# A prologue reordered in a Nyström attention and two-layer feed-forward kernel: query scores first, one weight quarter in two halves, one subtraction on another engine

## The chip, the cores and the metric

The kernel runs on one core of one Trainium2 chip. The metric is the time on the device in microseconds, and of several runs the median counts. The core has five engines that matter here: TensorE (PE in the profile, PEld for its weight loads), VectorE (DVE), ScalarE (ACT), GpSimd (POOL) and SyncE (SP), which issues the DMAs.

## What is computed

Three stages follow each other: Nyström attention over 4 batches of 8 heads (576 tokens of 64 values each), a SiLU layer with 2048 inner values, and a gated layer with RMS norm and 1536 inner values. The weights come as float64 and are turned into float32 on the chip.

```python
def _attn_ref(q, k, v):                      # m = 32 landmarks
    q_lm = q.reshape(B, H, m, S // m, D).mean(axis=3)
    k_lm = k.reshape(B, H, m, S // m, D).mean(axis=3)
    A = sm(q, k_lm)
    Bm = sm(q_lm, k_lm)
    C = sm(q_lm, k)
    Z = Bm.transpose(0, 1, 3, 2) / (norms of Bm + 1e-06)
    for _ in range(6):
        Z = 2 * Z - Z @ Bm @ Z
    return (A @ Z @ C @ v).astype(np.float32)

h = x @ w_in;  x = (h * sigmoid(h)) @ w_out
xn = x / rms * rms_g
out = (silu(xn @ w_gate) * (xn @ w_val)) @ w_out2
```

`sm` is a softmax of 0.125 times the product of its arguments, each row less its maximum.

## The kernel before, in words

**What is multiplied.** For each batch and each group `g` of four heads the attention makes two things: `at`, which is A (split into a rounded high part and a low part), and `lt`, a small 64 x 128 block that is Z, C and v multiplied out. The function `wprime(b, n)` multiplies `lt` into quarter `n` of w_in (512 columns), which gives the quarter `n` of the weights "wp" of that batch; the products `h` (L641) take `wp` and `at`. So nothing of the large products can start before `lt` of both groups of batch 0 is there, the first quarter of w_in is in float32, and `wprime(0, 0)` has run. That stretch of some 39 us is the prologue. After it PE runs the products `h` and `a` of the first layer, then the second layer.

**The prologue's attention.** `attention(ap, b, g, first)` is a generator; each `yield` ends a step. The two generators a0 and a1 (the two groups of batch 0, `first` true) are advanced in turn by the loop at the end of the function, a1 two steps behind a0. A step is: load q and k; load v; POOL sums the landmarks of q (L275 to L279); DVE sums those of k (`landmarks`, two TENSOR_REDUCE of kT, one for each half i); the key scores `pq` (L301, with k's landmarks as weights, needing all of q) and their transposes on DVE into `sa`; the query scores `c2` and then `c1` (L301, with q's landmarks as weights, needing all of k and its landmarks), six filler matmuls behind them for a1 (`idle`, L240), then the key maximum `ms` on DVE and the subtraction on POOL (L352); the query maximum on DVE (`mx`, then `nb`); the exponentials `bb` and `ec` on ACT; sums and reciprocals; `p1`, the norm and the first `rt`, and the transposes `ct` of `ec` (L408); copies of `ct`, the exponential of `sa`, and its sums; `pu` (L425), the rest of `rt`, and `sa` scaled on POOL (L429); six iterations `pe` (L308), each with a copy back (by DVE for a0, by ACT for a1) and a filler; at last `pl` and `lt` (DVE). In iteration 1 DVE transposes `sa` into `sb`, in iteration 2 ACT rounds it into the high part of `at`, in iteration 3 POOL subtracts that for the low part (L458).

**The conversion of w_in.** `load_win(n, g)` loads one quarter of one group (1 MB of float64) and `to_f32` converts it in blocks of 512 values: two ACT instructions (L163, L164) and two DVE instructions (L168, L170) a block, so eight and eight for the first quarter. Of L168 and L170 both inputs lie in SBUF, as both inputs of L458, L429 and L352 do. `load_wout(f)` does the same for a row block of w_out.

**What sets the order.** The framework puts each engine's instructions in one order at compile time, by program order shifted by `high_priority(offset)`, by a model of when each can run, and by `issue_after`, which keeps an instruction behind another on its engine. Each engine then runs its list in order. The dictionary `CONV` says behind which step t of the prologue's loop a conversion goes on (before: steps 11 to 20; entry 0 and 1 are the two groups' w_in, 2 is the first block of w_out). DMAs go to SP's queue in program order: q and k of both groups, w_in of group 0, v of both groups, w_in of group 1, four blocks of w_out, the second quarter of w_in.

**After the attention.** `wprime(0, 0)` issues its 16 matmuls (L478, two passes of 8, 512 columns), six fillers, and then in cuts of 256 columns ACT rounds `wp` (L486) and DVE subtracts (L487). Behind its last subtraction come the rest of the conversions of w_out's first four blocks, then w_in's second quarter, which `wprime(0, 1)` needs after the fifth step of the first layer.

Of the kernel before, what the change touches and what calls it, by code (L numbers as in the profile page):

```python
# [45 lines left out]
CONV = {11: (0,), 13: (0, 1), 14: (0,), 15: (0,), 16: (0, 2), 17: (1,), 18: (1,), 19: (1,), 20: (1,)}  # L46
# [20 lines left out]
def nystrom_moe_kernel(ctx: ExitStack, tc: tile.TileContext, q, k, v, w_in, w_out, w_gate, w_val, w_out2, rms_g, out):  # L67
# [130 lines left out]
    def load_win(n, g):  # L198
        raw = wslot(f"winr_{g}_{n}", [P, 2, 1024], I32)
        SP.dma_start(out=raw, in_=win_v[g, n].rearrange("c p f -> p c f"))  # L200
        yield
        t = nslot(2 * n + g, f"win_{g}_{n}", [P, 2, 512])
        size = (512, 512) if n < 2 else (1024, 1024)
        yield from to_f32(t.rearrange("p c f -> p (c f)"), raw.rearrange("p c f -> p (c f)"), *size)
        win_t[g, n] = t

# [35 lines left out]
    def attention(ap, b, g, first):  # L242
# [92 lines left out]
        sa = ht("sa", [P, R, M])  # L335
        for hf in range(2):
            pq = pa.tile([P, HB], F32, tag="a", name=f"pq_{n}_{hf}") if first else ps(f"pq_{n}_{hf}", [P, HB])
            scores(pq, kT, qT, 9 * hf, 9 * hf + 9)
            VE.transpose(sa[:, 9 * hf:9 * hf + 9].rearrange("p r j -> p (r j)"), pq)
        yield  # L340

        r1 = 10
        c1 = ps(f"c1_{n}", [P, r1 * M])
        c2 = ps(f"c2_{n}", [P, (R + 1 - r1) * M])
        for ci, (lo, hi) in ((c2, (r1, R + 1)), (c1, (0, r1))):
            x = scores(ci, qT, kT, lo, hi)
        if first and g:
            idle(x, 6)
        ms = sm("ms", [P, R])
        msb = ms.unsqueeze(2).to_broadcast([P, R, M])  # L350
        VE.tensor_reduce(ms, sa, axis=AX.X, op=ALU.max)
        (POOL if b <= POOL_B else VE).tensor_tensor(sa, sa, msb, op=ALU.subtract)  # L352
        yield
        nc2 = (R - r1) * M
        mx = sm("mx", [P, 4])
        nb = sm("nb", [P, 2])
        VE.tensor_reduce(mx[:, 2:3], c2[:, nc2:], axis=AX.X, op=ALU.max)
        VE.tensor_scalar(nb[:, 1:2], mx[:, 2:3], -0.125 / R ** 2, None, op0=ALU.mult)
        VE.tensor_reduce(mx[:, 1:2], c2[:, :nc2], axis=AX.X, op=ALU.max)
        VE.tensor_reduce(mx[:, 0:1], c1, axis=AX.X, op=ALU.max)  # L360
        VE.tensor_scalar(nb[:, 0:1], mx[:, 0:1], mx[:, 1:2], -0.125 / R, op0=ALU.max, op1=ALU.mult)
        yield
        ec = ht("ec", [P, M, R])
        ecv = ec.rearrange("p l r -> p r l")
        bb = sm("bb", [P, 2, M])
        su = sm("su", [P, 3])
        with ExitStack() as es:
            if first:
                es.enter_context(tc.high_priority(offset=EXP_PRIO))
                AE.activation(bb[:, 0], c2[:, nc2:], AF.Exp, bias=nb[:, 1:2], scale=0.125 / R ** 2, accum_out=su[:, 2:3])  # L370
                AE.activation(ecv[:, r1:], c2[:, :nc2].rearrange("p (r l) -> p r l", l=M), AF.Exp, bias=nb[:, 0:1], scale=0.125 / R, accum_out=su[:, 1:2])
                AE.activation(ecv[:, :r1], c1.rearrange("p (r l) -> p r l", l=M), AF.Exp, bias=nb[:, 0:1], scale=0.125 / R, accum_out=su[:, 0:1])
            else:
                es.enter_context(tc.issue_after(now[-1][0].ins))
                x = AE.activation(ecv[:, r1:], c2[:, :nc2].rearrange("p (r l) -> p r l", l=M), AF.Exp, bias=nb[:, 0:1], scale=0.125 / R, accum_out=su[:, 1:2])
                with tc.issue_after(x.ins):
                    AE.activation(bb[:, 0], c2[:, nc2:], AF.Exp, bias=nb[:, 1:2], scale=0.125 / R ** 2, accum_out=su[:, 2:3])
                    AE.activation(ecv[:, :r1], c1.rearrange("p (r l) -> p r l", l=M), AF.Exp, bias=nb[:, 0:1], scale=0.125 / R, accum_out=su[:, 0:1])
                    AE.activation(sa, sa, AF.Exp, scale=0.125 / R)
        yield  # L380
# [50 lines left out]
        for it in range(6):  # L431
# [38 lines left out]
    def wprime(b, nb_, prio=0):  # L470
# [4 lines left out]
        for i in range(4):  # L475
            for g in range(NG):
                hr = slice(64 * g, 64 * g + 64)
                x = PE.matmul(pw[g][32 * i:32 * i + 32], lts[b][hr, i], win_t[i // 2, nb_][hr, i % 2], start=True, stop=True)  # L478
        if (b, nb_) == (0, 0):
            idle(x, 6)  # L480
# [426 lines left out]
    early = [load_win(0, g) for g in range(NG)] + [load_wout(f) for f in range(EARLY)] + [load_win(1, g) for g in range(NG)]  # L907
    for gn in (a0, a1, early[0], a0, a1, *early[1:]):
        next(gn)
    t = 0  # L910
    live = [a0]
    while live:
# [4 lines left out]
        for n in CONV.get(t, ()):  # L917
            with tc.issue_after(VE.last.ins), tc.issue_after(AE.last.ins):
                next(early[n], None)
    with tc.issue_after(VE.last.ins):  # L920
        for gn in early[:NG]:
# [9 lines left out]
    with tc.issue_after(AE.last.ins):  # L931
        next(early[NG])
        for gn in early[NG + 1:NG + EARLY]:
            next(gn)
    z = wprime(*todo.pop(0), WP_PRIO)
    with tc.issue_after(z.ins):
        for gn in early[NG:NG + EARLY]:
            finish(gn)
    jobs = {f"n1{g}": gn for g, gn in enumerate(early[NG + EARLY:])}
# [196 lines left out]
```

## Time and profile before

| what | us |
|---|---|
| median of 3 runs (lowest, highest) | 881.53 (880.26, 884.51) |
| the profiled execution | 879.2 |
| its span in the profile | 877.4 |
| PE busy | 843.8 (96%) |
| DVE busy | 510.0 (58%) |
| ACT busy | 440.6 (50%) |
| POOL busy | 147.6 (17%) |

Busy shares are averages over stages with different limits. PE is near its limit over the whole span, and less so in the first 39 us, where it does small matmuls and fillers. A line of the timeline reads: start, duration, engine, line of the kernel, operation, output and inputs by the program's names, shape, how many instructions are merged, and in brackets how long the engine sat idle before it and what ended that.

### The profile page before, as it was taken

What the parts mean: (1) busy time and instruction counts of PE and PEld (TensorE: products, weight loads), DVE (VectorE), ACT (ScalarE), POOL (GpSimd) and SP (SyncE); (2) the same over time, 40 slices, a digit from 0 to 9 for tenths busy, and PEclk for the clock granted to TensorE, in tenths of its full rate; (3) what the DMA queues carried; (4) which work ended last, traced back from release to release, by engine and by line L of the source; (5) the groups of instructions that cost most, each with busy time, mean ns of one, the idle gap of its engine ahead of it and who ended that gap; (6) DMA issues with size and microseconds to landing.
All of it is one profiled execution on the core that took longest, in us unless ns stands there. A gap on an engine that the chain in (4) does not pass through costs nothing.

```text
span 877.4 us, 15413 instructions
## 1 busy us (share of the span) xinstructions
PE 843.8 (96%) x5896; PEld 735.9 (84%) x5896; DVE 510.0 (58%) x1038; ACT 440.6 (50%) x906; POOL 147.6 (17%) x171
## 2 busy tenths in 40 slices
PE   6899999999988999899989999999999999999996
PEld 3667766988876889889979888999989999999995
DVE  6878736786557647649853569733458434333332
ACT  3796523776556757656653346633445323232222
POOL 5200210223231222163740003300000000000000
PEclk9999999999998999999999999999999999999999
DMA  9788647128886569986895456758645557655543
GB/s 317 278 302 306 236 163 218 57 85 270 289 268 197 150 207 349 329 311 242 307 398 201 183 200 208 273 219 305 228 174 213 216 216 256 235 198 190 194 186 72
DMA packets 72586, 202.85 MB, mean 231 GB/s; under 512 B 6593, under 2 KB 34241, under 8 KB 68545
## 3 DMA queue, kind: packets, MB, share of 16 engines
q1 hardware_dynamic: 72512, 201.88, 65.4%
q8 instruction: 46, 0.75, 0.3%
q14 instruction: 28, 0.22, 0.1%
HBM read 149.29 MB, written 52.56 MB: 230 GB/s over the span
## 4 chain that ended last, share of the span: by engine, by line
PE 79%; DMA 6%; DVE 6%; ACT 5%; issue 2%; POOL 1%; SPq 0%; ACTq 0%; DVEq 0%; POOLq 0%
PE ga L815 17%; PE o L889 17%; PE a L661 11%; PE h L641 10%; PE gc L815 8%; PE a L658 7%; PE gb L815 4%; PE pw L478 2%; DMA w7d<-w7p 2%; PE pe L308 1%; DMA r_o<-in_moe_w_out_dram 1%; DMA r_v<-in_moe_w_val_dram 1%; DMA w<-w7d 1%; PE pq L301 1%; DVE lms L179 1%
## 5 line engine op out<-in xcount | busy, mean ns | idle before, releaser
L889 PE MATMUL o<-oc,u 128*128 128x512 f32 x648 | 178.9, 394 | 0.0
L661 PE MATMUL a<-hl,wo 128*128 128x288 f32 x1152 | 171.7, 298 | 2.5 <-DVE e L689 1.9
L815 PE MATMUL ga<-x,w 128*128 128x384 f32 x840 | 171.2, 338 | 2.3 <-DMA w<-w7d 1.2
L815 PEld LDWEIGHTS ga<-x,w 128*128 128x128 f32 x840 | 150.8, 188 | 16.6 <-ACT a L179 2.0
L661 PEld LDWEIGHTS a<-hl,wo 128*128 128x128 f32 x1152 | 159.8, 190 | 4.4 <-ACT hl L145 2.1
L641 PE MATMUL h<-at,wp 128*128 128x288 f32 x768 | 134.3, 310 | 3.3 <-ACT s L648 2.4
L641 PEld LDWEIGHTS h<-at,wp 128*128 128x128 f32 x768 | 110.1, 190 | 27.4 <-issue 7.8
L889 PEld LDWEIGHTS o<-oc,u 128*128 128x128 f32 x648 | 118.9, 188 | 13.0 <-DVE u L146 0.3
L179 DVE TENSOR_TENSOR v<-u,gc 128x384 f32<-128x384 f32 x72 | 39.6, 551 | 120.7 <-PE gc L815 120.5
L815 PE MATMUL gc<-x,w 128*128 128x384 f32 x420 | 84.8, 336 | 0.0
L815 PEld LDWEIGHTS gc<-x,w 128*128 128x128 f32 x420 | 74.8, 188 | 3.1
L146 POOL TENSOR_TENSOR hl<-s,hl 128x288 fp32r<-128x288 f32 x54 | 48.4, 898 | 146.6 <-ACT hl L145 120.6
L179 ACT COPY u<-ga 128x384 f32<-128x384 f32 x72 | 34.5, 479 | 71.4 <-PE ga L815 71.1
L179 DVE TENSOR_TENSOR u<-z,v 128x384 f32<-128x384 f32 x72 | 40.3, 560 | 50.9 <-ACT z L179 50.0
L658 PE MATMUL a<-s,wor 128*128 128x288 f32 x256 | 69.8, 409 | 0.0
L145 ACT CAST u<-u 128x384 fp32r<-128x384 f32 x72 | 36.9, 513 | 65.1 <-DVE u L179 65.1
L648 ACT ACTIVATE s<-h 128x288 f32<-128x288 f32 x96 | 38.9, 409 | 53.1 <-PE h L641 50.8
L146 DVE TENSOR_TENSOR u<-u,u 128x384 fp32r<-128x384 f32 x72 | 40.1, 557 | 29.6 <-ACT u L145 29.3
L658 PEld LDWEIGHTS a<-s,wor 128*128 128x128 f32 x256 | 45.8, 189 | 11.9 <-issue 1.7
L179 ACT ACTIVATE z<-ga 128x384 f32<-128x384 f32 x36 | 17.7, 492 | 73.9 <-PE ga L815 73.7
L551 POOL TENSOR_TENSOR t<-fw 128x256 f32<-128x256 f32 x24 | 22.7, 965 | 139.0 <-ACT x L779 81.4
L815 PE MATMUL gb<-x,w 128*128 128x384 f32 x210 | 42.3, 335 | 0.8 <-DVE v L179 0.8
(175 smaller groups left out, 1069.3 us busy)
## 6 DMA issues: line engine op xcount, KB each, us to landing
w<-w7d SPq DMA_DIRECT2D x31, 1792.0 KB, 7.3
oc<-wod SPq DMA_DIRECT2D x32, 512.0 KB, 7.9
win<-wind SPq DMA_DIRECT2D x20, 512.0 KB, 6.6
fw<-w2d SPq DMA_DIRECT2D x12, 768.0 KB, 6.8
winr<-in_moe_w_in_dram SPq DMA_DIRECT2D x8, 1024.0 KB, 7.0
wor<-in_moe_w_out_dram SPq DMA_DIRECT2D x16, 512.0 KB, 7.0
w7d<-w7p SPq DMA_DIRECT2D x16, 512.0 KB, 5.4
r_v<-in_moe_w_val_dram SPq DMA_DIRECT2D x12, 512.0 KB, 4.4
```

The lines of the kernel that those rows point to most:

```text
L145: x = ACT.copy(dst[:, 0], src) if hi is ACT else hi.tensor_copy(dst[:, 0], src)
L146: return x, lo.tensor_tensor(dst[:, 1], src, dst[:, 0].bitcast(F32), op=ALU.subtract)
L179: self.last = getattr(self.eng, name)(*args, **kw)
L301: x = PE.matmul(out[o], lm[y, i, R], t[y, i, lo:hi], start=True, stop=True)
L478: x = PE.matmul(pw[g][32 * i:32 * i + 32], lts[b][hr, i], win_t[i // 2, nb_][hr, i % 2], start=True, stop=True)
L551: POOL.tensor_tensor(t[:, to], x, y, op=ALU.subtract)
L641: PE.matmul(ph, w[:, x, fo:fo + P], a[:, y, tk], start=i == 0, stop=i == 5)
L648: ACT.activation(s, ph, AF.Silu)
L658: PE.matmul(acc[d], w[:, y], hl, start=start, stop=stop)
L661: PE.matmul(acc[d], w[:, x, y], hl[:, z], start=start and i == 0, stop=stop and i == 2)
L815: mm[0] = PE.matmul(acc, w7[:, x, o, kk], xs[:, y, kk], start=start and n == 0, stop=stop and n == 5, skip_group_check=True)
L889: PE.matmul(oacc[n], hls[j][:, x, t * P:(t + 1) * P], w[:, y], start=f == 0 and i == 0, stop=f == NF2 - 1 and i == 2)
```

## The change

In the attention of the first batch the query scores, their maximum (at high priority) and their exponentials come first, and the key scores, their transposes and their maximum behind them; a step less is needed. The subtraction for the low part of `at` (L458) goes from POOL to DVE for batch 0 (for batch 1 it stays on POOL, and later batches have it on DVE already). The first quarter of w_in is loaded in four DMAs of 256 of its 512 columns each, the first halves of both groups ahead of v and the second halves behind it, and it is converted in these halves, from step 8 to step 16 of a loop that is a step shorter; the ACT part of the first half stands ahead of the loop. `wprime(0, 0)` does the matmuls, the rounding and the subtraction for the first 256 columns and then for the others, with the six fillers between. The first DVE instruction on w_out's first block (L168) goes from ahead of `wprime(0, 0)` to behind it. Batches 1 to 3 keep the order of their scores.

```diff
-CONV = {11: (0,), 13: (0, 1), 14: (0,), 15: (0,), 16: (0, 2), 17: (1,), 18: (1,), 19: (1,), 20: (1,)}
+CONV = {8: ((1, 0),), 9: ((0, 0),), 10: ((0, 0),), 11: ((1, 0), (0, 1)), 12: ((1, 0), 0), 13: ((0, 1), (1, 1)), 14: ((0, 1),), 15: ((1, 1),), 16: ((1, 1),)}
...
+    def load_win0(x):
+        for g in range(NG):
+            if not x:
+                raw0.append(wslot(f"winr_{g}_0", [P, 2, 1024], I32))
+                win_t[g, 0] = nslot(g, f"win_{g}_0", [P, 2, 512])
+            y = slice(2 * x, 2 * x + 512)
+            SP.dma_start(out=raw0[g][:, :, y], in_=win_v[g, 0].rearrange("c p f -> p c f")[:, :, y])
+
+    def conv_win0(g, x):
+        raw, c = raw0[g][:, :, 2 * x:2 * x + 512], win_t[g, 0][:, :, x:x + 256]
...
+        ACT.activation(c, hi.bitcast(F32), AF.Abs, scale=2.0 ** -112)
+        ACT.activation(lo, raw.bitcast(U16).rearrange("p c (f t) -> p c f t", t=4)[:, :, :, 1], AF.Copy, scale=2.0 ** -13, bias=2.0 ** -14 - 0.5)
+        yield
+        DVE.scalar_tensor_tensor(out=lo, in0=hi, scalar=-0x80000000, in1=lo, op0=ALU.bitwise_and, op1=ALU.bitwise_or)
+        yield
+        DVE.scalar_tensor_tensor(out=c.bitcast(I32), in0=c.bitcast(I32), scalar=3, in1=lo, op0=ALU.logical_shift_left, op1=ALU.bitwise_or)
...
+        if first:
+            c1, c2, x = query_scores()
+            if g:
+                idle(x, 6)
+            with tc.high_priority(offset=EXP_PRIO):
+                query_max()
+            yield
+            with tc.high_priority(offset=EXP_PRIO):
+                ec, bb = exps()
+            key_scores()
+            yield
+            key_max()
+            yield
...
-                (POOL if b <= POOL_B else VE).tensor_tensor(at[:, 1], sb, at[:, 0].bitcast(F32), op=ALU.subtract)
+                (POOL if b == POOL_B else VE).tensor_tensor(at[:, 1], sb, at[:, 0].bitcast(F32), op=ALU.subtract)
...
         cut = W0 if (b, nb_) == (0, 0) else 512
-        with tc.high_priority(offset=prio):
-            for x in range(0, 512, cut):
-                y = slice(x, x + cut)
+        for x in range(0, 512, cut):
+            y = slice(x, x + cut)
+            for i in range(4):
+                for g in range(NG):
+                    hr = slice(64 * g, 64 * g + 64)
+                    z = PE.matmul(pw[g][32 * i:32 * i + 32, y], lts[b][hr, i], win_t[i // 2, nb_][hr, i % 2, y], start=True, stop=True)
+            if cut < 512 and not x:
+                idle(z, 6)
+            with tc.high_priority(offset=prio):
                 for g in range(NG):
                     ACT.copy(t[:, g, 0, y], pw[g][:, y])
                     z = DVE.tensor_tensor(t[:, g, 1, y], pw[g][:, y], t[:, g, 0, y].bitcast(F32), op=ALU.subtract)
...
-    for gn in (a0, a1, early[0], a0, a1, *early[1:]):
+    next(a0)
+    next(a1)
+    load_win0(0)
+    next(a0)
+    next(a1)
+    load_win0(256)
+    for gn in early:
         next(gn)
+    halves0 = {(g, x): conv_win0(g, 256 * x) for g in range(NG) for x in range(2)}
+    next(halves0[0, 0])
...
-        next(early[NG])
-        for gn in early[NG + 1:NG + EARLY]:
+        for gn in early[1:EARLY]:
             next(gn)
```

## Rows read from the trace of the kernel before

**Rows 1.** The page, busy time of each engine (share of the span) and instructions.
```profile
PE 843.8 (96%) x5896; PEld 735.9 (84%) x5896; DVE 510.0 (58%) x1038; ACT 440.6 (50%) x906; POOL 147.6 (17%) x171
```

**Rows 2.** The chain that ended last, first 70 us: start, us, what.
```profile
27.40 1.65 DVE winr L168
...
31.33 1.82 DVE wor L168
```

**Rows 3.** Timeline, 6 to 12 us: landmarks and the scores of a0.
```profile
6.56 2.17 DVE L179 TENSOR_REDUCE kT<-kT 128x32 f32<-128x576 f32 x2 [6.56 <-DMA kT<-in_k_dram]
...
8.32 0.32 POOL L279 TENSOR_TENSOR qT<-qs 128x64 f32<-128x64 f32 x1
...
9.60 1.15 DVE L179 TENSOR_REDUCE kT<-kT 128x32 f32<-128x576 f32 x1 [0.88 <-DMA kT<-in_k_dram]
...
9.75 0.69 PE L301 MATMUL c<-kT,qT 64*32 64x288 f32 x2
...
11.43 1.09 DVE L179 TENSOR_REDUCE kT<-kT 128x32 f32<-128x576 f32 x1
...
11.53 0.43 PE L301 MATMUL c<-kT,qT 64*32 64x320 f32 x2
```

**Rows 4.** Timeline, 13 to 19 us: scores of a1, exponentials of a0 and a1.
```profile
13.34 1.42 PE L301 MATMUL c<-kT,qT 64*32 64x288 f32 x12
...
13.76 1.28 ACT L179 ACT_TABLE_LOAD   x1 [13.76 <-DVE nb L179]
...
14.69 1.66 PE L240 MATMUL spare<-mean_w 128*128 128x512 f32 x6
...
15.33 0.73 ACT L179 ACTIVATE ec<-c,nb 128x256 f32<-128x256 f32 x1
...
16.81 0.91 PE L408 MATMUL ct<-ident,ec 128*96 128x128 f32 x6 [0.45 <-ACT ec L179]
...
18.60 0.86 ACT L179 ACTIVATE ec<-c,nb 128x320 f32<-128x320 f32 x1
```

**Rows 5.** Timeline, 20 to 34 us: DVE and POOL in the iterations.
```profile
20.95 0.33 DVE L179 TENSOR_SCALAR rt<-pu,rc,ic 128x64 f32<-128x64 f32 x1
...
25.27 1.41 POOL L429 TENSOR_TENSOR sa<-sa,ms 128x576 f32<-128x576 f32 x1 [2.30 <-DVE ms L179]
...
26.02 1.20 DVE L170 SCALAR_TENSOR_TENSOR win<-win,winr 128x512 int32<-128x512 int32 x1
...
26.73 1.77 POOL L458 TENSOR_TENSOR at<-sb,at 128x576 fp32r<-128x576 f32 x1
...
27.32 1.73 DVE L168 SCALAR_TENSOR_TENSOR winr<-winr 128x512 int32<-128x512 int32 x1
...
30.84 1.77 POOL L458 TENSOR_TENSOR at<-sb,at 128x576 fp32r<-128x576 f32 x1 [2.34 <-ACT at L179]
...
31.25 1.91 DVE L168 SCALAR_TENSOR_TENSOR wor<-wor 128x512 int32<-128x512 int32 x1
```

**Rows 6.** The page, groups: a DVE subtraction of the same kind, second layer.
```profile
L146 DVE TENSOR_TENSOR u<-u,u 128x384 fp32r<-128x384 f32 x72 | 40.1, 557 | 29.6 <-ACT u L145 29.3
```

**Rows 7.** Timeline, 35.5 to 42 us: lt of a1, wprime(0, 0), the first products.
```profile
35.85 1.54 PE L478 MATMUL pw<-win,lt 64*32 64x512 f32 x16
35.95 0.29 DVE L179 TENSOR_SCALAR lt<-pl 64x128 f32<-64x128 f32 x1 [0.47 <-PE pl L464]
...
37.90 1.62 DVE L487 TENSOR_TENSOR wp<-pw,wp 128x256 fp32r<-128x256 f32 x4 [1.65 <-ACT wp L486]
...
38.81 3.32 PE L641 MATMUL h<-at,wp 128*128 128x288 f32 x24
```

**Rows 8.** Timeline, 39 to 49 us: DVE's conversions, and wprime(0, 1) behind them.
```profile
39.44 0.68 DVE L170 SCALAR_TENSOR_TENSOR wor<-wos,wor 128x512 int32<-128x512 int32 x1
...
47.67 1.28 DVE L170 SCALAR_TENSOR_TENSOR win<-win,winr 128x512 int32<-128x512 int32 x2
...
48.41 0.14 PEld L478 LDWEIGHTS pw<-win,lt 64*32 64x32 f32 x4 [0.89 <-DVE win L170]
```

More of the change, by code (lines that the diff above doesn't have):

```diff
@@ L333, in attention @@
         yield
[L335 to L340, printed above, removed]
-        r1 = 10
[L343 to L346, printed above, removed]
@@ L347, in attention @@
-        if first and g:
-            idle(x, 6)
+        r1 = 10
+        nc2 = (R - r1) * M
         ms = sm("ms", [P, R])
         msb = ms.unsqueeze(2).to_broadcast([P, R, M])
[L351 to L354, printed above, removed]
         mx = sm("mx", [P, 4])
         nb = sm("nb", [P, 2])
-        VE.tensor_reduce(mx[:, 2:3], c2[:, nc2:], axis=AX.X, op=ALU.max)
-        VE.tensor_scalar(nb[:, 1:2], mx[:, 2:3], -0.125 / R ** 2, None, op0=ALU.mult)
@@ L380, in attention, with key_scores, query_scores @@
-        yield
+        su = sm("su", [P, 3])
+        sa = ht("sa", [P, R, M])
+        def key_scores():
+            for hf in range(2):
+                pq = pa.tile([P, HB], F32, tag="a", name=f"pq_{n}_{hf}") if first else ps(f"pq_{n}_{hf}", [P, HB])
+                scores(pq, kT, qT, 9 * hf, 9 * hf + 9)
+                VE.transpose(sa[:, 9 * hf:9 * hf + 9].rearrange("p r j -> p (r j)"), pq)
+        def query_scores():
+            c1, c2 = ps(f"c1_{n}", [P, r1 * M]), ps(f"c2_{n}", [P, (R + 1 - r1) * M])
+            for ci, (lo, hi) in ((c2, (r1, R + 1)), (c1, (0, r1))):
+                x = scores(ci, qT, kT, lo, hi)
+            return c1, c2, x
@@ new lines, in key_max, with query_max @@
+        def key_max():
+            VE.tensor_reduce(ms, sa, axis=AX.X, op=ALU.max)
+            (POOL if b <= POOL_B else VE).tensor_tensor(sa, sa, msb, op=ALU.subtract)
+        def query_max():
+            VE.tensor_reduce(mx[:, 2:3], c2[:, nc2:], axis=AX.X, op=ALU.max)
+            VE.tensor_scalar(nb[:, 1:2], mx[:, 2:3], -0.125 / R ** 2, None, op0=ALU.mult)
+            VE.tensor_reduce(mx[:, 1:2], c2[:, :nc2], axis=AX.X, op=ALU.max)
+            VE.tensor_reduce(mx[:, 0:1], c1, axis=AX.X, op=ALU.max)
+            VE.tensor_scalar(nb[:, 0:1], mx[:, 0:1], mx[:, 1:2], -0.125 / R, op0=ALU.max, op1=ALU.mult)
@@ new lines, in exps @@
+        def exps():
+            ec = ht("ec", [P, M, R])
+            ecv = ec.rearrange("p l r -> p r l")
+            bb = sm("bb", [P, 2, M])
+            x = [(bb[:, 0], c2[:, nc2:], nb[:, 1:2], R ** 2, su[:, 2:3]),
+                 (ecv[:, r1:], c2[:, :nc2].rearrange("p (r l) -> p r l", l=M), nb[:, 0:1], R, su[:, 1:2]),
+                 (ecv[:, :r1], c1.rearrange("p (r l) -> p r l", l=M), nb[:, 0:1], R, su[:, 0:1])]
+            pins = [] if first else [now[-1][0]]
+            for i in (0, 1, 2) if first else (1, 0, 2):
+                o, c, bias, r, acc = x[i]
+                with ExitStack() as es:
+                    for y in pins:
+                        es.enter_context(tc.issue_after(y.ins))
+                    z = AE.activation(o, c, AF.Exp, bias=bias, scale=0.125 / r, accum_out=acc)
+                    pins = pins if first else [z]
+            if not first:
+                with tc.issue_after(z.ins):
+                    AE.activation(sa, sa, AF.Exp, scale=0.125 / R)
+            return ec, bb
@@ new lines, in attention @@
+        if first:
[11 more added lines that the diff above has]
+            yield
+        else:
+            key_scores()
+            yield
+            c1, c2, x = query_scores()
+            key_max()
+            yield
+            query_max()
+            yield
+            ec, bb = exps()
+            yield
@@ L918, in nystrom_moe_kernel @@
             with tc.issue_after(VE.last.ins), tc.issue_after(AE.last.ins):
-                next(early[n], None)
+                next(early[n] if n == 0 else halves0[n], None)
     with tc.issue_after(VE.last.ins):
-        for gn in early[:NG]:
+        for gn in halves0.values():
             finish(gn)
```

36 lines of the change are left out of this document (7 added, 29 removed).

## The prediction, made before the changed kernel was run

> **What bounds the kernel now.** I read the page's busy times first: PE is busy 96% of the span [rows 1], so a change that touches only the prologue can bring no more than the start of the large products, which PE then runs nearly without a break. Next the chain that ended last: up to 39 us it goes through DVE far more often than through PE, and its longest DVE pieces are two conversions of 1.65 and 1.82 us [rows 2] that elsewhere take 0.68 us [rows 8]. Then the timeline of these 39 us: the first product `h` starts at 38.81 us [rows 7], 2.57 us after `lt` of a1 (35.95 + 0.29 = 36.24). So the forecast is: when does `lt` of a1 come now, does `h` follow it at the same distance, and does what waits behind it keep up.
>
> The profiled execution took 879.2 us for a span of 877.4; the median of the runs shown is 881.5, so 2.3 us more. I make the sum against 879.2 and add 2.3.
>
> **Query scores first.** They need q's landmarks (POOL, done at 8.32 + 0.32 = 8.64) and k's (DVE, 6.56 + 2.17 = 8.73) [rows 3]. Before, they ran from 9.75 to 11.96, 2.2 us, mixed with the key scores. Started at 8.73 they end near 10.9. DVE has a1's k landmarks to do (it starts on them at 9.60, when k lands; 1.15 and 1.09 us) and the query maximum of a0, which I take at 1.2 us (five instructions; 320 columns of it are 0.47 and the rest is less). Whichever comes first, a0's maximum is done between 12.0 and 13.1. The exponentials `ec` of a0 started at 15.33 [rows 4], behind a table load of 1.28 us; they would start 2.2 to 3.3 us sooner, the load being ahead of the conversion's ACT part, which is now ACT's first work.
>
> That is not the gain, because PE is next. In the new program order a1's query scores, six fillers and a1's key scores stand ahead of a0's transposes `ct`. a1's landmarks are done between 11.9 and 13.1; then scores of 1.4 us (12 matmuls [rows 4]), fillers of 1.65, key scores of 1.4 again: PE is free for `ct` between 16.3 and 17.6, against 16.81 before [rows 4]. So `ct` of a0 gains 0.5 or loses 0.8. What a0 does gain is behind it: before, its second copy of `ct` and its exponential stood behind a1's `ec` on ACT, which ended at 19.46 (18.60 + 0.86); these now come some 2 us sooner. For the moment `rt` of a0 is complete (20.95 before [rows 5]) I take 0.7 us sooner, between a loss of 0.8 and a gain of 2.2 (what the exponentials gain at least). The clearer gain, a1's exponentials, serves a chain that must also follow a0's matmuls on PE.
>
> **`at`'s low part on DVE.** Two stalls show the price of the old place [rows 5]. The POOL subtraction from 26.73 to 28.50 leaves the DVE conversion of 27.32 unfinished until 29.05, 0.55 us behind POOL's end; the one from 30.84 to 32.61 holds that of 31.25 until 33.16, again 0.55 behind it. With 0.68 as the undisturbed time these two lost 1.05 and 1.23 us, 2.3 together, and both pieces are on the chain [rows 2]. The third, 1.20 us at 26.02, ended 0.54 us behind POOL's multiplication of 25.27, which stays. Against that DVE gets two subtractions of 576 columns: 557 ns for 384 [rows 6] make 0.84 each, 1.7 together; by the conversion's 0.68 for 512 they are 0.77 each, 1.5. Net gain 0.6 to 0.8; 0.7 taken. On DVE the subtraction waits for ACT's rounding of the high part; behind it stand the next conversion and a0's next copy back, for which its iteration waits. The conversions ahead of it cover that wait; without them it would cost up to ACT's one instruction.
>
> *A rule that speaks against it.* The conversion of 26.02 shows that POOL's other instructions collide with DVE's as well, where both sides read two inputs from SBUF. The change puts the conversions from step 9 on, beside POOL's four instructions of L352 and L429 over 576 columns, which stay, and puts two more such subtractions on DVE. If two of the conversions lose what that of 27.32 lost, 1.05 us each, the gain turns into a loss of 1.4. The Trainium skill says this (SBUF — State Buffer, section "SBUF: two separate sides"): DVE with two SBUF inputs and a GpSimd instruction lock a shared port pair for the whole instruction, and the loser waits. By that rule, the trace agrees: both held conversions ended the same 0.55 us behind POOL.
>
> **w_in in halves.** Four DMAs of 512 KB for two of 1 MB: the same bytes in all, and v behind as many bytes as before. At worst the halves land when the whole quarters did, which the kernel before bore; at best nobody needs them sooner, since PE and DVE are what the steps wait for. I cost it, and the two more issues on SP, at nothing both ways; were that cover gone, v would delay `pu`. The eight ACT and eight DVE conversions stay eight and eight, of the same size; they only stand earlier. All of them are still ahead of `lt`, so the halves take no DVE work out of the prologue. Only w_out's L168 goes behind: 0.68 us undisturbed (its other 1.23 are counted above).
>
> **`wprime(0, 0)` in halves.** All but the first of the sixteen matmuls ran from 36.3, when `lt` of a1 was there, to 37.39 [rows 7]. The halves take about 0.55 us each, with the six fillers (1.66 [rows 4]) between: PE still spends 2.7 us ahead of `h`. Nothing gained, at most 0.2 lost by the extra weight loads. DVE's last subtraction, though, now waits for the second half: before it ended at 37.90 + 1.62 = 39.52, 3.3 us after `lt`; now the second half's matmuls end 2.8 after `lt`, the first subtraction comes 0.5 behind them as before (37.39 to 37.90), and two take 0.8: 4.1. That is 0.8 later.
>
> **Who is queued behind that.** DVE converts w_out's four blocks and w_in's second quarter without a gap from 39.44 to 48.95 [rows 8], and `wprime(0, 1)` on PE waited 0.89 us for the last of them. Now this row of work starts 0.8 us later, counted from `lt`, and is 0.68 longer. PE can lose 1.5 us there; it loses nothing if the order on PE puts other products ahead. The row of 0.89 is nearest; 0.9 us taken.
>
> **The sum.** Gains at `lt`: 0.7 (order of the scores) + 0.7 (`at` on DVE) + 0.7 (w_out's L168) = 2.1; I add 0.4 of the 2 us and more that a1's exponentials gain, the rest of which waits on PE behind a0's work: 2.5. Less 0.9 at `wprime(0, 1)`: 1.6 us. 879.2 - 1.6 = 877.6 for an execution like the profiled one, and 879.9 with the 2.3 of the median. Ends: gains of 2.2 + 0.8 + 0.7 + 0.9 and nothing given back make 4.6 (876.9); a loss of 0.8 at `ct`, of 1.4 by collisions, of 0.2 for the matmuls and of 1.5 behind `lt`, less L168's 0.7, make a loss of 3.2 (884.7).
>
> About 0.5%, 4.4 us, is what a measurement of this kernel can tell from no change; 1.6 us is no change by that.
>
> **The rivals.**
> 1. *Both chains gain in full.* a1's exponentials come over 2 us sooner, a0's too, DVE is never held, and the later work keeps up. For it: DVE is the longest part of the chain up to 39 us, and its work shrinks. Against it: PE's order ahead of `ct`, and the dense row of conversions behind `lt`. 876.9.
> 2. *The planner keeps the old order, so the change does not do what it says.* The key scores can run from the first half of k's landmarks on, 7.6 us, a microsecond before the query scores [rows 3], and PE is idle then. If they are put first, the exponentials gain little, the 0.7 of the first term falls away and so does the 0.4: 879.9 + 1.1 = 881.0.
> 3. *Collisions move instead of going.* As worked out above, two held conversions turn +0.7 into -1.4: 879.9 + 2.1 = 882.0.
> 4. *The backlog behind `lt` decides: slower.* `lt` comes no sooner because `ct` of a0 waits for a1's fillers and key scores on PE, and the conversions end 1.5 us later. PE reaches `wprime(0, 1)` with the weights missing; its matmuls, of which the last waited for DVE before already [rows 8], wait 1.5 us and break into one or two more pieces. 0.8 for `ct`, 1.5, and up to 1.1 for each further piece, what the whole took [rows 7]: 3.4 to 4.5, so 884.9 to 886.0. It decides where PE is free for `ct` later than 16.81 and DVE's last conversion of w_in's second quarter ends later than 48.95. Against it: the planner sees the backlog and can put other products first.
>
> **How the numbers follow.** Forecast (between 0.5 and 3.5 us faster) 0.45; rival 1 0.22, of it 0.17 past 0.5%; rival 2 0.13; rival 3 0.10; rival 4 0.10, of it 0.07 past 0.5%. So faster 0.17, same 0.76, slower 0.07. The range leaves out half of rivals 1 and 4 and reaches over the others: 876.3 to 883.2. The three runs before already lie 4.2 us apart, so a narrower one would not hold.
>
> **What would show it.** Right, step by step: c of a0 starts by 9 us and `ec` of a0 by 13; no DVE conversion over 1.3 us from 26 us on; the DVE subtraction of `at` at 0.77 to 0.84 us; `lt` of a1 near 33.7 and the first `h` 2.5 to 2.7 us behind it; DVE dense for some 13 us after the last L487 and PE waiting at L478 about as long as before or a microsecond longer. Wrong: `lt` before 32 or after 36, an `h` more than 3 us behind `lt`, or a difference that grows in the products after 60 us, for which nothing here gives a reason.

## The result: 0.95% slower, and the profile after

| | before | after |
|---|---|---|
| median of 10 runs each, on one chip, us | 882.31 | 889.80 |
| lowest, highest | 876.30, 884.89 | 886.14, 892.84 |
| ratio, 95% interval (of the two medians alone: 1.0085) | | 1.0095, 1.007 to 1.012 |
| profiled execution: span, us | 877.4 | 889.0 |
| mean granted clock of TensorE | 0.992 | 0.976 |
| first `h`, us | 38.81 | 51.52 |

The forecast was 879.9, no change, in a range from 876.3 to 883.2. The change is slower, outside the range, and on the side that the prediction gave 0.07. The medians lie 7.5 us apart. The two profiled executions lie 11.6 us apart in their spans, so what follows shows the loss somewhat larger than it is in the median; every "first `h`" below is read from one execution too. The kernels that keep the old order of the scores start the last matmuls of iteration 0 between 22.43 and 23.28 us, so differences of `h` below 1 us say little.

The page's busy times after (compare [rows 1]): PE's busy time grew by 10.8 us although it got only 16 instructions more, its weight loads' by 5.5; no other engine's grew by more than 1.0.

```profile
PE 854.6 (96%) x5912; PEld 741.4 (83%) x5912; DVE 511.0 (57%) x1040; ACT 440.7 (50%) x906; POOL 144.7 (16%) x169
```

Why it got longer stands in the windows of the kernel after: from, to, length, then busy time and instructions of PE, PEld, DVE, ACT and POOL, the granted clock of PE, DMA share, GB/s.

```profile
10.00:20.00 10.00, 8.79 (x105) 4.66 (x97) 8.63 (x30) 4.97 (x14) 4.11 (x8) 1.00 1.04 293
20.00:25.00 5.00, 5.00 (x51) 3.27 (x40) 1.86 (x6) 2.75 (x6) 0.00 (x0) 0.51 1.03 407
25.00:30.00 5.00, 3.47 (x87) 2.56 (x85) 4.31 (x13) 5.00 (x10) 2.57 (x2) 0.81 1.02 408
30.00:35.00 5.00, 3.24 (x51) 1.91 (x51) 5.00 (x12) 0.95 (x3) 1.41 (x1) 0.54 0.60 236
35.00:40.00 5.00, 5.00 (x60) 2.74 (x60) 2.79 (x6) 1.05 (x3) 0.00 (x0) 0.50 0.04 6
40.00:45.00 5.00, 5.00 (x66) 2.85 (x69) 1.17 (x3) 0.48 (x2) 0.00 (x0) 0.50 0.97 352
45.00:50.00 5.00, 5.00 (x40) 2.60 (x30) 1.05 (x3) 3.13 (x7) 0.00 (x0) 0.50 0.74 273
50.00:60.00 10.00, 9.87 (x66) 7.49 (x64) 7.91 (x15) 8.29 (x16) 0.00 (x0) 0.96 0.01 3
```

In the kernel before the clock was 1.00 (2.4 GHz) in each of these windows, here 20 to 30 us:

```profile
20.00:30.00 10.00, 7.79 (x183) 5.21 (x175) 8.80 (x22) 8.05 (x17) 4.33 (x3) 1.00 1.02 406
```

Now it is 0.50 (1.2 GHz) from 20.1 to 26.9 us and again from 30.4 to 50.9, some 27 of 31 us. Busy time alone hides this: from 35 to 50 us PE is "100% busy" in both kernels.

The timeline of the kernel after, 7 to 33 us, shows what came first (answers to [rows 3 to 5]):

```profile
7.72 2.69 PE L324 MATMUL pq<-qT,kT 64*32 64x288 f32 x14 [7.72 <-DVE kT L179]
...
9.74 0.69 PE L324 MATMUL c<-kT,qT 64*32 64x288 f32 x2
...
13.14 1.28 ACT L179 ACT_TABLE_LOAD   x1 [13.14 <-DVE nb L179]
...
14.71 0.73 ACT L179 ACTIVATE ec<-c,nb 128x256 f32<-128x256 f32 x1
...
16.80 0.69 PE L460 MATMUL ct<-ident,ec 128*96 128x128 f32 x4
...
17.12 1.16 POOL L381 TENSOR_TENSOR sa<-sa,ms 128x576 f32<-128x576 f32 x1 [4.66 <-DVE rc L179]
17.15 1.17 DVE L179 TENSOR_SCALAR bb<-bb,rc 128x32 f32<-128x32 f32 x1
...
18.49 0.34 DVE L179 TENSOR_SCALAR bb<-bb,rc 128x32 f32<-128x32 f32 x1
...
18.71 0.26 PE L331 MATMUL p<-bb 32*32 32x32 f32 x8 [1.21 <-DVE bb L179]
...
21.59 0.63 PE L460 MATMUL ct<-ident,ec 128*96 128x128 f32 x2
...
22.25 0.85 DVE L179 STREAM_TRANSPOSE sa<-pq 128x288 f32<-128x288 f32 x2 [1.92 <-PE ct L460]
...
24.28 0.34 DVE L179 TENSOR_SCALAR rt<-pu,rc,ic 128x64 f32<-128x64 f32 x1 [1.18 <-PE pu L477]
...
25.86 1.31 DVE L224 SCALAR_TENSOR_TENSOR winr<-winr 128x512 int32<-128x512 int32 x1
...
26.47 0.43 PE L331 MATMUL pe<-rt,nid 32*32 32x64 f32 x8
...
28.44 0.37 PE L331 MATMUL pe<-rt 32*32 32x96 f32 x8 [1.53 <-DVE rt L179]
...
31.53 0.54 PE L331 MATMUL pe<-rt 32*32 32x96 f32 x8 [1.16 <-DVE rt L179]
...
32.44 1.64 DVE L224 SCALAR_TENSOR_TENSOR winr<-winr 128x512 int32<-128x512 int32 x1
```

- The key scores of a0 still go first on PE (7.72), the query scores at 9.74 as before. The planner kept that, and the table load stayed in the path at 13.14, since the conversion's ACT part came no sooner than 23.10. `ec` of a0 gained 0.62 us.
- `bb` of a0, 0.34 us when free (that of a1), took 1.17 beside POOL's subtraction of the key maximum, which is now due at that moment, and ended 0.04 us behind it. PE stood still for 1.21 us.
- The two parts of `ct`, six matmuls in one row before, are now 4.8 us apart (16.80, 21.59). Fillers, `pq` and `ct` share four PSUM banks, and a1's key scores `pq` hold two of them until 22.25: their transposes into `sa` wait for the buffer of `ec`, which `ct` is the last to read. So the second part did not wait for these transposes, it ran ahead of them; PE's order has `p`, part of `pu` and four fillers in front of it. Which bank it got the rows don't show; that the buffer is what parts the two is shown below.
- `rt` of a0 is complete at 24.62 instead of 21.28, iteration 0 starts near 26.2, and then conversions, two of them held beside POOL (25.86, 32.44), and other work stand ahead of a0's copies on DVE (1.53 and 1.16 us of PE idle).

In the kernel before the last matmuls of iteration 0 were these:

```profile
22.43 0.29 PE L308 MATMUL pe<-rt,nid 32*32 32x64 f32 x8
```

The delay of 12.7 us at the first `h` in three stretches: the last matmuls of iteration 0 start at 26.47 instead of 22.43 (4.0); `lt` of a1 is there at 47.03 instead of 36.24 (6.8 more); from `lt` to `h` it takes 4.49 us instead of 2.57 (1.9 more), because the six fillers and the matmuls of `wprime(0, 0)` run at half clock (2.82 at full clock, in the halves with two fillers below). The timeline of the kernel after, 46 to 53 us, answers to [rows 7]:

```profile
46.74 0.29 DVE L179 TENSOR_SCALAR lt<-pl 64x128 f32<-64x128 f32 x1 [3.06 <-PE pl L516]
...
48.11 2.89 PE L263 MATMUL spare<-mean_w 128*128 128x512 f32 x6
...
50.93 0.66 PE L533 MATMUL pw<-win,lt 64*32 64x256 f32 x16
51.52 1.62 PEld L693 LDWEIGHTS h<-at,wp 128*128 128x128 f32 x12 [0.41 <-issue]
```

The theories to be told apart: **order** (waits in the order of DVE and of the buffers make the chain late) and **clock** (the gaps let TensorE's clock fall, and everything up to `h` runs at half speed).

### The profile page after: what moved, and what is told of

The parts are those of the page before. It is cut to its first block, busy times and chain, and to the rows that moved or that the text cites. A ratio compares the mean times of both kernels' runs of the same rounds, so it can differ in the third digit from the quotient of the medians.

```text
span 889.0 us, 15447 instructions
## 1 busy us (share of the span) xinstructions
PE 854.6 (96%) x5912; PEld 741.4 (83%) x5912; DVE 511.0 (57%) x1040; ACT 440.7 (50%) x906; POOL 144.7 (16%) x169
## 4 chain that ended last, share of the span: by engine, by line
PE 79%; DMA 8%; DVE 5%; ACT 5%; issue 1%; POOL 1%; SPq 0%; ACTq 0%; DVEq 0%; POOLq 0%
PE o L941 16%; PE ga L867 16%; PE a L713 12%; PE h L693 10%; PE gc L867 8%; PE a L710 7%; PE gb L867 4%; PE pw L533 2%; PE pe L331 2%; DMA wor<-in_moe_w_out_dram 1%; DMA w2d<-r_o 1%; DMA w<-w7d 1%; PE spare L263 1%; DMA winr<-in_moe_w_in_dram 1%; DMA r_o<-in_moe_w_out_dram 1%
## 5 line engine op out<-in xcount | busy, mean ns | idle before, releaser
L146 DVE TENSOR_TENSOR u<-u,u 128x384 fp32r<-128x384 f32 x72 | 40.1, 557 | 30.6 <-ACT u L145 30.4
```

Of the source, the lines that this page charges most:

```text
L146: return x, lo.tensor_tensor(dst[:, 1], src, dst[:, 0].bitcast(F32), op=ALU.subtract)
```

## Experiments

### The three parts, each alone

In the kernel before, `at`'s low part on DVE:

```diff
-                (POOL if b <= POOL_B else VE).tensor_tensor(at[:, 1], ...
+                (POOL if b == POOL_B else VE).tensor_tensor(at[:, 1], ...
```

> The kernel before with one part of the change: the low part of `at` for batch 0 on DVE. Theory A (the new score order opens a gap on PE near 18 us, TensorE's granted clock falls to half there and stays low until 51 us): the order of the scores is the old one, so the clock stays at 1.00 from 14 to 36 us, and the time is 0 to 1.5 us below before (ratio 0.998 to 1.000). Rival B (the subtractions on DVE hold back the copies of the iterations, PE starves and the clock falls with it): the clock falls after 25 us and the time is 4 us or more above before (ratio over 1.004).

The new order of the scores alone (the conversions a step earlier, since the loop is a step shorter):

> The kernel before with the new order of the scores alone (the conversions' steps moved up by one, since the loop is a step shorter). Theory A: the second part of `ct` of a0 comes after 20 us, PE has a gap of about 1 us before `p`, the granted clock is near 0.5 from 21 us on, the first h comes after 46 us; ratio 1.006 to 1.011, as the whole change. Rivals B and C (the subtraction on DVE, or the halves of w_in): the clock stays at 1.00 and the ratio is 0.996 to 1.002.

The halves of w_in and of `wprime(0, 0)` alone, with the change's conversion steps (one later, 9 to 17, as the loop has its old length):

> The kernel before with the halves of w_in's first quarter and of wprime(0, 0) alone (old score order, subtraction on POOL, the conversions' steps moved back by one). Theory A: the clock stays at 1.00 to 36 us, the first h within 1.5 us of before, ratio 0.998 to 1.003. Rival C (the halves bring the conversions forward to where they hold DVE, and PE starves): a clock of 0.5 in some stretch between 20 and 45 us and a ratio over 1.004.

| | ratio, 95% | first `h` | clock in the iterations |
|---|---|---|---|
| `at` on DVE | 0.9973, 0.9937 to 1.0009 | 38.66 | 1.00 |
| scores | 1.0052, 1.0023 to 1.0081 | 46.65 | half from 34.7 |
| halves | 1.0062, 1.0027 to 1.0098 | 45.90 | half from 29 |

Two parts cost; `at` costs nothing that can be measured and perhaps gains. Theory A was right on `at`. On the scores it had the loss about right, but not the clock, which held past the gap near 18 us and fell 14 us later than it said. On the halves it missed, and rival C came true. In both that cost, `h` of the profiled execution is 7 to 8 us late and the clock has fallen (the profiled execution of the halves took 892.95 us, the longest of its ten, whose median was 884.34). What preceded the fall, in the halves alone: DVE's timeline, 26 to 30 us.

```profile
26.91 0.67 DVE L224 SCALAR_TENSOR_TENSOR winr<-winr 128x512 int32<-128x512 int32 x1
...
27.69 0.62 DVE L226 SCALAR_TENSOR_TENSOR win<-win,winr 128x512 int32<-128x512 int32 x1
28.23 0.23 DVE L179 COPY rt<-pe 128x96 f32<-128x96 f32 x1
```

PE's timeline of the same kernel, 26 to 31 us:

```profile
28.52 0.37 PE L331 MATMUL pe<-rt 32*32 32x96 f32 x8 [1.08 <-DVE rt L179]
28.71 0.29 PE L331 MATMUL pe<-rt,id 32*32 32x64 f32 x8
28.93 0.75 PE L263 MATMUL spare<-mean_w 128*128 128x512 f32 x1
29.61 0.54 PE L331 MATMUL pe<-rt 32*32 32x96 f32 x8
29.93 0.43 PE L331 MATMUL pe<-rt,id 32*32 32x64 f32 x8
30.30 0.80 PE L263 MATMUL spare<-mean_w 128*128 128x512 f32 x1
```

Two conversions stand ahead of the copy of 28.23; PE waits 1.08 us, and from 29 us on the same shapes take 0.54 instead of 0.37, 0.43 instead of 0.29 and 0.80 instead of 0.49. In the new order alone the last gap before the fall is of 2.48 us, before 33.15.

### The clock, by fillers

The iterations have one filler each, none in iteration 0. Without any, in the kernel before:

```diff
-                if it:
-                    idle(x, 1)
```

> The kernel before without the single fillers of the iterations, nothing else; no part of the change is in it. Theory A: the granted clock falls to 0.5 in the iterations (after 24 us), the first h comes after 44 us and the ratio is 1.006 to 1.012: the fall of the clock alone costs what the change cost. Rival: the fillers only cost PE time, the chain shortens and the ratio is below 1.000.

1.0009 (0.9977 to 1.0041), a miss for both: the clock fell, but only late (32 to 42 us), `h` came at 42.00, and the total doesn't show it; the interval leaves room for these 3.2 us. With two in every iteration, in the kernel after, in the kernel with `at` alone, in that with the halves alone and in the kernel before:

```diff
-                if it:
-                    idle(x, 1)
+                idle(x, 2)
```

> The whole change with the extra fillers in the iterations only, the gap near 18 us left as it is. Theory A: the clock may still fall near 20 us, as in the changed kernel, but the iterations bring it back or hold it; first h between 38 and 48 us, ratio between that of f_gap and 1.009. Rival: no change against the changed kernel, 1.008 to 1.011.

> The kernel before with the low part of `at` on DVE and two fillers instead of one (none in iteration 0) in the iterations. Theory A: the clock is 1.00 through the prologue in more of the runs than with the subtraction alone; ratio 0.993 to 0.998. Rival: the fillers lengthen PE's chain by 3 us or more, ratio over 1.001.

> The kernel before with the halves alone (conversions at steps 9 to 17), and two fillers in each iteration instead of one, iteration 0 too. Theory 'clock' (the halves' whole loss is TensorE at half clock in the iterations; the gaps of about 1 us by themselves are cheap): the clock stays at 1.00 or comes back before 31 us, iterations of 0.9 to 1.1 us, first h at 39.5 to 42 us (two fillers in the kernel with at's part on DVE cost 1.9 us), ratio 1.000 to 1.003. Theory 'order' (DVE's conversions ahead of the copies delay the chain whatever the clock): the clock may be back, but first h stays at 43.5 to 46 us and ratio 1.004 to 1.007.

> The kernel before with two fillers in every iteration, nothing else. Theory 'fillers only cost where the clock held anyway': clock 1.00 in the prologue, first h at 39.8 to 41.2 us, ratio 1.000 to 1.004. Rival 'the kernel before loses its clock in some executions, and the fillers cure that': ratio 0.995 to 0.998, with the higher of the times gone.

| two fillers an iteration in | ratio, 95% | without them | first `h` |
|---|---|---|---|
| before | 0.9998, 0.9943 to 1.0054 | 1 | 41.14 |
| `at` alone | 1.0003, 0.9979 to 1.0027 | 0.9973 | 40.58 |
| halves alone | 0.9993, 0.9963 to 1.0024 | 1.0062 | 41.12 |
| after | 1.0085, 1.0051 to 1.0119 | 1.0095 | 47.09 |

`at` alone came out between its two theories, the others as their first theory said, the whole change only in its wide bounds. The halves tell most. Windows of the halves alone, one filler:

```profile
28.00:30.00 2.00, 1.48 (x29) 0.95 (x33) 2.00 (x4) 0.38 (x2) 2.00 (x2) 0.75 1.03 391
30.00:32.00 2.00, 2.00 (x30) 1.22 (x22) 1.84 (x4) 0.83 (x2) 1.80 (x2) 0.50 1.02 410
```

The same windows with two fillers:

```profile
28.00:30.00 2.00, 1.58 (x35) 0.92 (x34) 2.00 (x4) 0.50 (x2) 2.00 (x2) 1.00 1.02 389
30.00:32.00 2.00, 1.98 (x36) 1.00 (x30) 2.00 (x5) 0.81 (x2) 1.81 (x2) 1.00 1.04 416
```

The clock holds, `h` comes within 0.02 us of the control's 41.14, and no loss is left that can be measured. So the halves themselves (DMAs, `wprime` in two passes) cost nothing beyond the noise (0.9993, at most 1.0024); **their loss came by way of the clock**. In the kernel after, the clock was back at 26.5 us, before the first of these fillers (26.94; without them it was back at 26.9 too). What they did is hold it from there on: `h` came 4.4 us sooner, at 47.09, yet the ratio hardly moved (the two intervals leave room for a gain of 4 us). What is left with the clock held is order: iteration 0 started at 26.72, and PE waited 1.14, 0.93 and 0.56 us for a0's copies. Fillers between `ct` and `p` as well, where the first gap stands:

```diff
...
+            if first and not g:
+                es.enter_context(tc.issue_after(idle(ct_part(0, 4), 4).ins))
...
```

> The whole change with more fillers on PE: four between the first part of `ct` of a0 and `p`, where PE stood still, and two instead of one (none in iteration 0) behind each iteration's matmuls. Theory A (the loss is TensorE's clock, which falls in PE's gaps of the prologue): granted clock 1.00 in all stretches from 14 to 36 us, first h before 40 us, ratio 0.996 to 1.003, although PE has some 20 fillers (about 5 us) more to run. Rival (the new order itself delays lt by its waits on DVE and buffers, and the clock only follows): the clock is held, yet the first h comes after 44 us and the ratio stays over 1.005.

1.0073 (1.0037 to 1.0109), a miss for Theory A, and the rival's `h` and ratio without the held clock that it asked for: iteration 0 came 3.1 us sooner (23.36), with the clock at 1.00 until then, yet it was at half from 27 to 37 us, behind a gap of 2.06 us, and `h` came at 47.39. So of the 4.0 us by which iteration 0 is late in the kernel after, about 1 is waits and 3 the half clock from 20.1 on. Fillers alone do not mend the change.

### The order

First one buffer: `sa` of a1 in a buffer of its own, in the kernel after.

```diff
-        sa = ht("sa", [P, R, M])
+        sa = nslot(4, f"sa_{n}", [P, R, M]) if first and g else ht("sa", [P, R, M])
```

> The whole change, but a1's `sa` has a buffer of its own instead of waiting until `ec` of a0 is read, so that a1's key scores are transposed and their PSUM banks come free earlier. Theory A with the buffers as the cause: the second part of `ct` of a0 follows the first before 18 us, the clock stays at 1.00 to 36 us, the first h comes before 38 us and the ratio is 0.995 to 1.001. If the buffers are not the cause but the filler order or the wait of `p` for `bb` is, the gap and the fall of the clock stay and the ratio is 1.005 or more.

1.0103 (1.0048 to 1.0157, four runs). Both parts of `ct` now stand at 17.29, so the buffer is what had parted them, and still iteration 0 came at 25.49: `bb` was held all the same (0.90 us), and DVE came to `rt` only at 24.91 (1.48 us of PE idle). The wait for the buffer was real, but others stood right behind it. Next, the halves alone with conversions three steps later:

> The kernel before with w_in's first quarter in halves alone, and the conversions three steps later in the loop than in the earlier run with the halves (steps 12 to 20, where the kernel before has 11 to 20). Theory 'order' (the halves cost only because their conversions stand ahead of a0's copies on DVE, and the gap that this tears into TensorE's work brings the clock down): the copies of the iterations come at once, no gap over 0.7 us ahead of a0's matmuls pe, clock 1.00 through the iterations, first h at 38.5 to 40.5 us, ratio 0.998 to 1.002. Rival 'the halves themselves' (four smaller DMAs, v later, wprime(0, 0) in two passes): first h still at 44 us or later and ratio 1.005 to 1.008.

1.0053 (1.0015 to 1.0092), `h` at 46.93: a miss for "order" as it was put, and the numbers are those of the rival, which the run with two fillers rules out. No conversion stands ahead of the copies up to 27.4 us any more. The gap of 1.26 us ahead of `pe` is one that the kernel before has too (before 23.98, at a clock of 1.00). That of 0.98 comes from another DVE instruction, held beside POOL's subtraction for `at` of a0 (25.71 to 27.11):

```profile
26.03 1.12 DVE L179 TENSOR_SCALAR ms<-ms 128x18 f32<-128x18 f32 x1
```

And the clock fell at 26.3 us, before that second gap, behind nearly the same PE work through which the kernel before kept it (10.57 us busy in the 12.3 us up to 26.3, against 10.59 in the 12.3 us up to 25.89, each in 188 matmuls). So the gaps that PE had had by then do not by themselves explain the fall. Then the key part moved as a whole: the own buffer, and the key maximum with POOL's subtraction behind the first part of `rt`, on the new order alone.

```diff
-            key_max()
...
         for (i0, i1) in ((0, 4), (4, 6)):
...
+        if first:
+            with tc.issue_after(VE.last.ins):
+                key_max()
```

> The kernel before with the new order of the scores alone, with a1's sa in a buffer of its own, and the key maximum and POOL's subtraction put behind the first part of rt on DVE. Theory 'key part' (the new order costs because POOL's subtraction holds bb, because a1's key scores keep their PSUM banks from a0's second part of ct, and because the key maximum stands ahead of bb): bb of a0 takes under 0.4 us, both parts of ct by 18 us, rt of a0 complete by 21 us, iteration 0 by 21.5, first h by 39.5, ratio 0.996 to 1.001. Rival 'PE's order' (a1's query scores, six fillers and key scores ahead of ct of a0, and p behind them, cost the same whatever DVE does; or the late key part comes due at at): rt of a0 complete after 22.5 us or at late, first h at 42 us or later, ratio 1.004 to 1.008.

And the same in the kernel after with its conversions two steps later, with one filler, then with two:

> The changed kernel with these repairs together: the conversions two steps later, a1's sa in a buffer of its own, the key maximum and subtraction behind the first part of rt. at's low part stays on DVE, the halves stay. If the loss is order alone, both repairs add up: clock 1.00 through the iterations, first h by 39.5 us, ratio 0.994 to 1.000 (at's part on DVE had 0.997 alone). If the parts cost through something else, or the late key part crowds DVE in the iterations: gaps over 1 us ahead of pe of a0, clock at half, first h at 43 us or later, ratio 1.004 to 1.010.

> The changed kernel with the three repairs of order (conversions two steps later, a1's sa in a buffer of its own, the key part behind the first part of rt) and two fillers in every iteration. Theory 'order and clock, nothing else': iteration 0 at 22.5 us as with the repairs alone, the clock at 1.00 or back at it before 32 us, first h at 40.5 to 42.5 us (22.5 and the 18.4 us that the halves with these fillers took from iteration 0 to h), ratio 0.998 to 1.003. Rival 'something else of the change costs too' (conversions held by POOL or queued on DVE, the backlog of conversions behind lt): first h later than 43.5 us, or an h in time and a ratio of 1.005 or more.

| | ratio, 95% | iteration 0 | first `h` |
|---|---|---|---|
| scores, key part later | 1.0029, 0.9993 to 1.0065 | 22.21 | 45.93 |
| after, all three repairs | 1.0081, 1.0049 to 1.0113 | 21.84 | 47.51 |
| the same, two fillers | 1.0066, 1.0002 to 1.013 (four runs) | 21.98 | 45.41 |

("Iteration 0" is the start of its last matmuls, 22.43 before.) The late start is gone in all three, and `h` still comes 6.6 to 8.7 us late: the theory that the repairs mend the loss missed three times (the first of the three can't be told from no change). The gap had moved into the iterations, and the clock fell there, with two fillers too (29.9 to 36.7 us). POOL's timeline in the repaired kernel with two fillers:

```profile
28.21 1.41 POOL L483 TENSOR_TENSOR sa<-sa,ms 128x576 f32<-128x576 f32 x1 [1.44 <-DVE ms L179]
```

DVE's timeline of the same kernel and moment:

```profile
28.52 1.65 DVE L224 SCALAR_TENSOR_TENSOR winr<-winr 128x512 int32<-128x512 int32 x1
30.09 0.24 DVE L179 COPY rt<-pe 128x96 f32<-128x96 f32 x1
```

The conversion, 0.6 to 0.7 us when free, ended 0.55 us behind POOL, as in [rows 5], and a0's copy stood behind it. Last, then, the conversions six steps later than in the change (steps 14 to 22), with two fillers and with one:

> The changed kernel with the repairs of order and two fillers an iteration as before, but the conversions six steps later than in the change (steps 14 to 22), so that none stands ahead of a0's copies of iterations 0 to 3. Theory 'order and clock, nothing else': no gap over 0.8 us ahead of a0's matmuls pe, clock 1.00 through the iterations, first h at 40 to 42 us, ratio 0.997 to 1.003. Rival 'something else': clock kept and still first h after 43.5 us, or h in time and a ratio of 1.005 or more.

> The same with one filler an iteration, none in iteration 0. If the order alone now keeps the clock: first h at 38 to 40 us, ratio 0.995 to 1.001, the best version of the change. If the waits that are left still bring the clock down: half clock from the iterations on, first h at 43 us or later, ratio 1.003 to 1.008; the difference to the run with fillers is then the price of the clock alone.

| after, repaired, conversions late | ratio, 95% | iteration 0 | first `h` |
|---|---|---|---|
| two fillers | 1.0004, 0.9971 to 1.0036 | 21.99 | 39.34 (four; the rest from 40.71) |
| one filler | 1.0038, 1.0009 to 1.0067 | 22.15 | 42.03 (four; the rest from 43.57) |

Windows of the version with two fillers:

```profile
30.00:32.00 2.00, 2.00 (x45) 1.11 (x36) 1.98 (x4) 0.91 (x2) 0.00 (x0) 1.00 1.03 410
32.00:34.00 2.00, 2.00 (x37) 1.08 (x28) 1.49 (x3) 0.58 (x2) 0.00 (x0) 1.00 0.51 197
```

The same windows with one:

```profile
30.00:32.00 2.00, 0.39 (x17) 0.27 (x16) 2.00 (x5) 0.81 (x2) 0.00 (x0) 1.00 1.02 408
32.00:34.00 2.00, 2.00 (x27) 1.13 (x20) 1.66 (x4) 0.69 (x2) 0.00 (x0) 0.63 0.45 168
```

With both mended, the changed kernel can't be told from the kernel before (0.9971 to 1.0036): what is left of the change costs nothing that can be measured. With one filler a gap of 1.61 us is left (`sb` waits for POOL's multiplication, `at`'s subtraction and a conversion follow, all ahead of a0's copy), the clock falls behind it, and 2.7 us at `h`, 3.0 in the median of ten, are lost; the intervals of the two ratios overlap.

### A version that might beat both

The kernel before with `at` on DVE and a filler in iteration 0 as well:

```diff
-                if it:
-                    idle(x, 1)
+                idle(x, 1)
```

> The kernel before with at's low part on DVE and one filler in iteration 0 too (the kernel before has one in iterations 1 to 5 alone). If a filler in iteration 0 keeps the clock without standing in the chain: first h at 38.5 to 39.5 us, clock 1.00 in the prologue, ratio 0.995 to 0.999. If it stands in the chain, or there is nothing to keep: ratio 0.998 to 1.002, as at's part alone (0.997, from 0.994 to 1.001).

0.9977 (0.9927 to 1.0028): the clock held and `h` came at 38.21, the earliest of all, but there is no difference that can be measured. No version here is shown to be faster than the kernel before.

## Why the prediction was wrong

- **Query scores first: the wrong step.** The prediction asked when PE would be free for `ct` (16.3 to 17.6; it was 16.80, right) and took "0.7 us sooner, between a loss of 0.8 and a gain of 2.2" for the complete `rt`. It came 3.3 us later. What was put behind (transposes, key maximum, POOL's subtraction) was costed at nothing, as if deferred work went nowhere: it kept a PSUM bank from the second part of `ct` and met `bb` on DVE. These waits are about 1.3 of the 3.3 us: with the gap behind `ct` filled and the clock at 1.00, `rt` is complete at 22.56. The rest is the half clock that followed. The runs that moved the key part brought iteration 0 from 26.47 back to about 22. The prediction's own signs of being wrong came with it: `lt` after 36 (47.03) and `h` more than 3 us behind it (4.49).
- **w_in in halves, "nothing both ways": wrong in size.** Its DMAs and sizes do cost nothing (0.9993 with the clock held). The sentence "they only stand earlier" is what failed: earlier conversions stand ahead of a0's copies, PE waits for these, and in the run that lost, the clock fell behind such a wait. With later conversions it fell too, so that place alone is not the whole cause.
- **The clock is in no term of the sum.** A lost microsecond was taken as one microsecond. In the kernel after it is 0.50 for most of the stretch from 20 to 50 us; with order repaired, one filler against two shows its price, net of the fillers' own time: 2.7 us at `h` in one execution of each. What in a stretch of small matmuls decides whether it falls stays open.
- **`at` on DVE: borne out.** The subtraction took 0.75 us, a little less than the 0.77 to 0.84 predicted. `h` came only 0.15 us sooner, but that execution was 0.84 us later already at iteration 0: from there to `h` it took 15.39 us instead of 16.38. 0.9973 doesn't contradict 0.7 us (0.9992), and its interval doesn't exclude no gain. The section of the Trainium skill that the prediction cited (SBUF — State Buffer, "SBUF: two separate sides") held again: 1.65 us at 28.52, ending 0.55 behind POOL.
- **`wprime(0, 0)` in halves: about right** at full clock. From `lt` to `h` it takes 2.82 us in the halves with two fillers (2.57 before, and "at most 0.2 lost"); in the mended version four products start after 2.12 and the rest after 3.49. At half clock it is 4.49.
- **Behind `lt`.** `wprime(0, 1)` broke into three pieces as rival 4 said, with waits of 0.39 and 0.16 us for DVE in the mended version too, which was no slower.
- **Rivals.** Rival 1 fell with its first step. Rival 2 was right that the planner keeps a0's key scores first, rival 3 that collisions move: the conversions of 25.86 and 32.44 lost 0.6 and 1.0 us to POOL, where it had two of 1.05. Neither gives 7.5 us. Rival 4 had the sign, not the cause: the loss was there before `lt`. Nothing was lost behind `h`: 12.7 us late there, 11.6 in the span.
- **The range** left out the prediction's own lower end (884.7) and the whole of rival 4 as it was priced (884.9 to 886.0), not half of it. The measured 889.8 lies beyond these too.

## What to carry to other kernels

Work that is put off needs its own account: which buffers and banks it holds until it is done, and whom it meets at its new time. On a chain of small matmuls, look at the granted clock in windows before and after any reordering; a microsecond of gap there can be followed by many at half clock, and a filler or two more per step show whether the clock is the cause. Compare parts with the clock held as well as without, or the same loss is blamed on each part in turn.

## What the runs showed of the hardware

- TensorE's clock fell in stretches with gaps of about 1 to 2.5 us between busy pieces (at 20.1 and 30.4 us in the kernel after, 29.0 in the halves alone, 34.7 in the new order alone). The gaps alone do not tell when: the kernel before stood idle for 2.2 of the 10 us from 20 to 30 and kept 1.00 in its profiled execution, the halves alone stood idle for 2.2 of the same 10 us and lost it. Where the limit lies these runs don't tell.
- At half clock it stayed while the rows show PE busy without a break, with one filler an iteration and small matmuls: from 35 to 50 us in the kernel after, from 30 to 45 in the halves alone. In the kernel after it came back twice: at 26.9 us, when PE had been busy since 18.7, and at 50.9, behind six fillers in a row. Two fillers an iteration kept it in the kernel before, in `at` alone and in the halves; in the repaired kernel it fell in spite of them at 29.9 and was back at 36.7.
- That the clock has two levels, as the Trainium skill says (TensorE: Matmul & The Clock Gate, section "Part 1: The HAM clock gate"), the windows bear out: 0.50 and 1.00, and values between them only where a window holds a change.
- Executions of one kernel differ, and the mean granted clock goes along with it: on one chip the kernel before took 874.5 to 879.3 us at a mean clock of 0.993 to 0.996, 880.6 at 0.989, and 883.5 to 886.6 at 0.979 to 0.983. It is not the clock alone: on another chip two executions at 0.991 took 875.9 and 883.1 us.
- Not only conversions are held by POOL: a DVE multiplication of one tensor by a factor per row (`bb`, 128x32) took 1.17 us instead of 0.34, and ended 0.04 us behind POOL's subtraction in the kernel after as in three runs that keep that order; with the subtraction moved away it took 0.20. The addition of a constant (`ms`, 128x18, 0.15 to 0.28 us elsewhere) took 1.12 us in the halves with later conversions, to 0.04 us behind POOL's subtraction.
